# Zero matmuls in the gaps of the first batches, score pieces of one full bank, and `x` written by chunks

## The chip, the cores and the metric

One core of a Trainium2 chip runs the kernel. The metric is the time of one execution on the device in microseconds, as the median of three runs. TensorE (PE) multiplies matrices; its weight loads are listed as PEld. VectorE (DVE), ScalarE (ACT) and GpSimd (POOL) do the rest, and the queues of SyncE (SP) and ACT issue the transfers. The clock of TensorE is granted at one of two levels, 1.2 or 2.4 GHz; the profile gives the granted share (0.50 or 1.00) of every stretch.

## What is computed

Eight batches of eight heads, 576 tokens of 64 numbers each, in fp32. First a linear attention with a norm; its result, laid out with 512 numbers a token, goes into a mixture of four attention experts, of which each token uses two.

```python
kv  = einsum('bhsd,bhse->bhde', k, v)
out = einsum('bhsd,bhde->bhse', q, kv)
x   = out / sqrt(mean(out*out, -1) + 1e-6) * g_norm     # -> [B, S, 512]
logits = x @ w_gate                                     # two best of four experts, softmax over them
for e in range(4):
    q, k, v = x @ wq[e], x @ wk[e], x @ wv[e]
    a = softmax(causal(q @ k.T / sqrt(64)))
    y += gate[e] * (a @ v @ wo[e])
```

## The kernel before

A batch goes through these steps, each a small function of the kernel that emits its instructions. `kv(b, c)` multiplies k and v of two heads in twenty instructions and four such pieces make a batch; `kvx` and `kvc` copy the result out of PSUM, `kt` and `kg` multiply it with the gate weights `wg_bd`. `q(b, i)` turns q over (five tiles of tokens, the last of 64 rows; in batches 0 and 1 on TensorE, later on VectorE), `out(b, i)` is the product with `kv`. `oc` copies it to `o_sb`, `sq` squares it on ACT, `red` sums on DVE, eleven small `nw` steps on DVE find the reciprocal root, and `xm(b, i)` on POOL scales the tile into `x_tok`. `x(b, i)` turns it over on TensorE in four transposes (L585), `xc` copies it to `xT`. Then the expert projections `v` (five tiles), `qp` and `kp` (for two pairs of experts), and for each pair the scores `sc`, in pieces of one PSUM buffer each, with `exp` on ACT and a causal mask `msk` on POOL per piece; `pv` multiplies with v, `rc`, `iv` and `oc2` scale, `ot` turns over, `otc` copies, `y` multiplies with wo, `yc` copies and `st` stores. The weights of the projections are loaded by `lw` and scaled by `ws`, k, v and q by `lk`, `lv`, `lq`, the gate weights by `lg0`.

All of this is written in an order that a planner makes before the kernel is built. `graph` lists the steps with their engine, an assumed duration, their needs and their buffers; `plan` takes, step by step, the one that can start first, and of those that can start within 0.025 of each other the one with the least `urgency`: a number per kind of step in `URGENCY`, plus `PERIOD` per batch, plus single corrections in `EDGES`. The engines then run their instructions in exactly this order. `SWAP` says for which steps the engine of a copy is exchanged. PSUM is divided into two small buffers of one bank (`sm`: kv, q, kt, kg, x, v, ot, y) and three large ones of two banks (`bg`: out, qp, kp, sc, pv). A matmul that writes a buffer waits until the step that read the buffer's earlier content has ended. Six SBUF buffers (`x`) hold both `x_tok` tiles and the weights as they are loaded.

## Time and profile before

| | |
|---|---|
| median of three runs | 261.76 us (261.53 to 261.89) |
| the profiled execution | 259.49 us, its span 257.8 us |
| TensorE busy | 228.5 us (89% of the span), 2456 matmuls |
| DVE, ACT, POOL busy | 169.7, 152.5, 82.6 us |
| mean granted clock of TensorE | 0.934 |
| moved by DMA | 40.28 MB, 156 GB/s over the span |

The profile is of one execution. Matmuls are pipelined and their ends are modelled, so a busy TensorE is not one at its peak; the chain of waits, which follows the work that ended last back from the end, shows how long a step held the next one up. Names of buffers stand as output, arrow, inputs.

### The profile page before, as it was taken

Reading aid. Unit: us, or ns where it says so; the run is one execution under the profiler, and the core shown is the slowest. Engines: PE = TensorE matmul, PEld = TensorE weight load, DVE = VectorE, ACT = ScalarE, POOL = GpSimd, SP = SyncE. Lnnn points to the kernel's source line nnn. Section 1 sums busy time; section 2 is a strip of 40 time slices with the busy share of each in tenths; the row PEclk is TensorE's granted clock in tenths of the full one; section 3 lists DMA queues with packets and bytes.
Section 4 is the critical chain, followed back from the end, with each engine's and each line's share of the span. In section 5 each row is a group of like instructions: output and inputs, shape, how many; then the busy total and the mean of one; then the engine's idle time right before and its main releaser. Section 6 shows DMA issues by size and latency. Waiting matters only on the chain.

```text
span 257.8 us, 6403 instructions
## 1 busy us (share of the span) xinstructions
PE 228.5 (89%) x2456; PEld 205.5 (80%) x2456; DVE 169.7 (66%) x503; ACT 152.5 (59%) x277; POOL 82.6 (32%) x160
## 2 busy tenths in 40 slices
...
DMA packets 99432, 40.28 MB, mean 156 GB/s; under 512 B 76618, under 2 KB 94538, under 8 KB 99402
## 3 DMA queue, kind: packets, MB, share of 16 engines
...
q8 instruction: 19, 0.31, 0.6%
...
## 4 chain that ended last, share of the span: by engine, by line
PE 78%; DMA 7%; DVE 6%; ACT 4%; SPq 1%; issue 1%; POOL 0%; DVEq 0%; POOLq 0%; ACTq 0%
PE p_out L630 15%; PE p_sc L814 9%; PE p_x L585 8%; PE p_q L788 7%; PE p_kv L567 7%; PE p_y L896 7%; PE p_v L770 7%; PE p_k L788 7%; PE p_pv L848 5%; DMA q_b<-in_q_dram 3%; DMA k_b<-in_k_dram 3%; ACT PT L828 2%; PE p_ot L886 2%; DMA w_stage<-in_moe_wv_dram 2%; PE p_kg L611 1%
## 5 line engine op out<-in xcount | busy, mean ns | idle before, releaser
L834 POOL TENSOR_SCALAR_AFFINE_SELECT PT<-PT 128x256 bf16<-128x256 bf16 (+1 forms) x80 | 29.3, 384 | 126.1 <-ACT PT L828 125.0
L828 ACT ACTIVATE PT<-p_sc 128x512 bf16<-128x512 f32 (+3 forms) x80 | 50.6, 718 | 3.4 <-PE p_sc L814 3.0
L709 POOL TENSOR_TENSOR x_tok<-o_sb,rs 128x512 f32<-128x512 f32 (+1 forms) x40 | 41.2, 1049 | 19.1 <-DVE rs L685 19.0
L630 PE MATMUL p_out<-kvx,qT 128*128 128x136 f32 x320 | 44.8, 290 | 0.9 <-DVE kvx L456 0.4
L630 PEld LDWEIGHTS p_out<-kvx,qT 128*128 128x128 f32 x320 | 41.2, 197 | 2.3 <-DVE o_sb L456 0.6
L814 PE MATMUL p_sc<-qTp,kT 128*128 128x288 f32 (+4 forms) x192 | 39.0, 323 | 0.0
L656 DVE TENSOR_REDUCE ms<-sq 128x8 f32<-128x520 f32 (+1 forms) x40 | 27.1, 687 | 17.7 <-ACT sq L650 17.2
L585 PE MATMUL p_x<-ident_f,x_tok 128*128 128x128 f32 (+1 forms) x160 | 28.3, 307 | 5.2 <-POOL x_tok L709 4.1
L650 ACT ACTIVATE sq<-o_sb 128x512 f32<-128x512 f32 (+1 forms) x40 | 25.0, 634 | 11.8 <-DVE o_sb L456 9.6
L814 PEld LDWEIGHTS p_sc<-qTp,kT 128*128 128x128 f32 x192 | 28.5, 190 | 3.6 <-ACT PT L828 0.7
L567 PE MATMUL p_kv<-v_b,k_b 128*64 128x64 f32 x512 | 23.4, 242 | 8.9 <-DMA k_b<-in_k_dram 7.8
L567 PEld LDWEIGHTS p_kv<-v_b,k_b 128*64 128x64 f32 x512 | 20.0, 153 | 12.4 <-issue 11.0
L456 DVE COPY o_sb<-p_out 128x544 f32<-128x544 f32 (+1 forms) x30 | 21.4, 716 | 11.2 <-PE p_out L630 11.0
L585 PEld LDWEIGHTS p_x<-ident_f,x_tok 128*128 128x128 f32 (+1 forms) x160 | 23.1, 209 | 7.1 <-POOL x_tok L709 5.5
L770 PE MATMUL p_v<-wv_r,xT 128*128 128x256 f32 x160 | 25.7, 292 | 0.7 <-DVE vext L456 0.7
L896 PE MATMUL p_y<-wo_b,OT 128*128 128x512 bf16 x80 | 23.8, 400 | 1.0 <-ACT OT L454 0.7
L454 ACT CAST kT<-p_k 64x576 fp32r<-64x576 f32 x32 | 20.3, 634 | 4.7 <-PE p_k L788 4.2
L770 PEld LDWEIGHTS p_v<-wv_r,xT 128*128 128x128 f32 x160 | 21.6, 189 | 1.6 <-DVE vext L456 1.1
L788 PE MATMUL p_q<-xT,wq_r 128*128 128x288 f32 x128 | 21.9, 323 | 0.0
L454 ACT CAST xT<-p_x 128x512 fp32r<-128x512 f32 (+1 forms) x25 | 13.3, 545 | 14.3 <-PE p_x L585 14.2
L788 PE MATMUL p_k<-xT,wk_r 128*128 128x288 f32 x128 | 20.2, 303 | 0.0
L788 PEld LDWEIGHTS p_q<-xT,wq_r 128*128 128x128 f32 x128 | 19.3, 206 | 0.3
...
## 6 DMA issues: line engine op xcount, KB each, us to landing
...
k_b<-in_k_dram SPq DMA_DIRECT2D x14, 512.0 KB, 5.2
v_b<-in_v_dram SPq DMA_DIRECT2D x14, 512.0 KB, 7.8
...
```

Source lines behind the costliest of these rows:

```text
L454: nc.scalar.copy(dst, src)
L567: nc.tensor.matmul(p_kv[hh * Dh : (hh + 1) * Dh, c, :], lhsT=lhs, rhs=rhs, start=(j == 0), stop=(j == NF), skip_group_check=True,)
L585: nc.tensor.transpose(p_t[:, c, :nt], chunk(c)[:nt], ident_f[:nt, :nt])
L630: nc.tensor.matmul(p_o[:, c // 2, (c % 2) * 256 : (c % 2) * 256 + 2 * GW], lhsT=blocks_of(qT, c)[:, i * P : (i + 1) * P], rhs=kvx[b % 2][: ...
L656: nc.vector.tensor_reduce(mss[b % 2][:nt, i, :], sqs[(NB * b + i) % 3][:nt], axis=AX_X, op=AluOpType.add)
L709: nc.gpsimd.tensor_tensor(out=buf(("x", b, i), [P, H, Dh], FP32, "x_tok")[:nt], in0=ob[:nt, i, :, 0:Dh], in1=st["rstd", b][:nt, i * H : (i ...
L770: nc.tensor.matmul(p_v[:], lhsT=blocks_of(xTs[b % 2], c)[:, i * P : (i + 1) * P], rhs=w_r["v"][:, c, :, :].rearrange("p e f -> p (e f)"), ...
L788: nc.tensor.matmul(p_p[:, s, 0:HALF], lhsT=w_r[nm][:, c, 2 * pr : 2 * pr + 2, :].rearrange("p e f -> p (e f)"), rhs=blocks_of(xTs[b % 2], ...
L814: nc.tensor.matmul(p_s[:, el, o : o + hi - lo], lhsT=kTs[pr][el][:, kb * P : (kb + 1) * P], rhs=tiles["qTp", b, pr][:, lo:hi], start=True, ...
L828: nc.scalar.activation(PT[:, :, d0 : d0 + o], big("sc", b, pr, j)[:, :, 0:o], ACTF.Exp, scale=scale)
L834: nc.gpsimd.affine_select(out=d, in_=d, compare_op=AluOpType.is_ge, fill=0.0, base=0, pattern=[[0, 2], [1, w]], channel_multiplier=-1,)
L896: nc.tensor.matmul(p_y[:], lhsT=blocks_of(OTs[b % 2], pr)[:, qc * P : (qc + 1) * P], rhs=wo_b[:, pr, :], start=(pr == 0), stop=(pr == EP - 1),
```

## The change

TensorE gets matmuls of zeros: in the planner's order, wherever it sees a gap ahead of a TensorE step in the first 55 us, as many as fill 0.8 of that gap (0.5 in the first 10 us) are written into the PSUM tile that the step is about to use, just ahead of it. There are 79 of them: 26, 4, 4 and 7 of 256 columns ahead of the four pieces of `kv(0)`, 2, 3, 3, 3 and 3 of 512 columns ahead of the tiles of `q(0)`, 2 ahead of the first `out(0)`, 13 of 256 columns between the halves of `kv(1)`, 4 of 512 ahead of the second tile of `q(1)`, and 2 and 3 ahead of the first two tiles of `x(0)`. POOL sets a tile of zeros for them before the first. The score pieces go from five to four a pair, with 512 columns per expert in three of them and 64 in the last; the mask steps follow. `xm` writes `x_tok` so that every fourth element of a token stands in one chunk of 128, and the transposes read such a chunk. In the last batch `ot` and `otc` run in two parts, tokens 0 to 383 and 384 to 575, and each `y` tile needs only its part. Copies are swapped between DVE and ACT one by one, two of the six `ws` go to DVE, and the numbers of the order are others.

```diff
-ON_ACT = ("kvc", "xc", "qpc", "kpc", "otc", "yc")
-SWAP = {"kgc": (6,), "ktc": (1,), "kvc": (0,), "kvx": (1,), "oc": (0, 1), "otc": (1,), "qc": (1,), "qpc": (7,), "vc": (1, 6), "xc": (0, 6, 7), "yc": (0, 1, 6)}
...
+SWAP = {
+    "ws": (('q', 0), ('v', 0),), "qc": ((0, 4), (1, 0), (1, 1), (1, 3),),
+    "oc": ((0, 0), (0, 1), (1, 2), (1, 3), (1, 4), (6, 1), (6, 2), (6, 3), (7, 2), (7, 3),),
+    "xc": ((0, 0), (0, 1), (1, 0), (1, 2), (1, 4), (6, 0), (6, 2), (6, 3), (7, 2), (7, 4),),
...
+                    name, nd = ("ws", nm, p), [("lw", nm, p), ("lg0",)]
+                    (dve if swapped(name) else pool)(name, 0.60 if swapped(name) else 1.08, nd, (("x", nm, p),))
...
-            hold = (0.31, 0.31, 0.46, 0.34, 0.46)
-            took = (0.66, 0.66, 0.95, 0.72, 0.60)
...
-            for j in R5:
-                pe(("sc", b, p, j), hold[j], [("qpc", b, p), ("kpc", b, p)], (("bg", "sc", b, p, j), ("qTp", b, p)))
-                act(("exp", b, p, j), took[j], [("sc", b, p, j)] + old, (("bg", "sc", b, p, j),))
-                if j != 1:
-                    pool(("msk", b, p, j), 0.41 if j < 4 else 0.70, [("exp", b, p, j)])
+            for j in R4:
+                pe(
+                    ("sc", b, p, j), (0.47, 0.62, 0.52, 0.24)[j], [("qpc", b, p), ("kpc", b, p)],
+                    (("bg", "sc", b, p, j), ("qTp", b, p)),
+                )
+                act(("exp", b, p, j), 1.09 if j < 3 else 0.28, [("sc", b, p, j)] + old, (("bg", "sc", b, p, j),))
+                pool(("msk", b, p, j), (0.41, 0.41, 0.80, 0.36)[j], [("exp", b, p, j)])
...
+            for at in ((b, p),) if b < B - 1 else ((b, p, 0), (b, p, 1)):
+                part = at[2] if at[2:] else 2
+                pe(
+                    ("ot",) + at, (0.20, 0.14, 0.31)[part], [("oc2", b, p, g) for g in R2 if g == part or part == 2],
+                    (("sm", "ot") + at, ("osc", b, p)),
...
-COLD = 15.005
+WARM = 55.0
+COLD = 6.005
...
-PERIOD = 173.5
+PERIOD = 171.6
 URGENCY = {
-    "den": (51.7, -21.4, -19.57), "ex": (292.1, 19.87, -23.53), "exp": (295.6, -38.9, -16.04),
...
+    "den": (-113, -5.12, -28.6), "ex": (-96.9, 40.06, -25.25), "exp": (1115.2, -48.08, -0.44),
...
+            if space is psum and dtype == FP32 and len(shape) < 4:
+                t = tiles[key][:]
+                keep_warm(t if len(shape) == 2 else t.rearrange("p a b -> p (a b)"))
...
+    def keep_warm(t):
+
+        n = min(512, t.shape[1])
+        for _ in range(int(idle[0] / (n / 2400.0 + 0.01)) if n >= 256 else 0):
+            nc.tensor.matmul(t[:, 0:n], lhsT=zeros[:, 0:P], rhs=zeros[:, 0:n], start=True, stop=True, skip_group_check=True)
+        idle[0] = 0.0
...
-        p_kv = small([P, NCH, Dh], "kv", b)
+        p_kv = small([P, 2, NCH, Dh], "kv", b)
+        keep_warm(p_kv[:, 1].rearrange("p c d -> p (c d)"))
+        p_kv = p_kv[:, 0]
...
+        shape = [nt, H, Dh // NCH, NCH]
         nc.gpsimd.tensor_tensor(
-            out=buf(("x", b, i), [P, H, Dh], FP32, "x_tok")[:nt],
-            in0=ob[:nt, i, :, 0:Dh],
-            in1=st["rstd", b][:nt, i * H : (i + 1) * H].unsqueeze(2).to_broadcast([nt, H, Dh]),
+            out=buf(("x", b, i), [P, NCH, P], FP32, "x_tok")[:nt].rearrange("p c (h r) -> p h r c", h=H),
+            in0=ob[:nt, i, :, 0:Dh].rearrange("p h (r c) -> p h r c", c=NCH),
+            in1=st["rstd", b][:nt, i * H : (i + 1) * H].unsqueeze(2).unsqueeze(3).to_broadcast(shape),
...
-        t = tiles["x", b, i][:].rearrange("p h d -> p (h d)")
-        transpose_in(i, lambda c: t[:, c : c + NCH * (P - 1) + 1 : NCH], "x", b, i)
+        transpose_in(i, lambda c: tiles["x", b, i][:, c, :], "x", b, i)
...
-    PIECES = (((0, 0, HALF),), ((0, HALF, S),), ((1, P, S),), ((2, 2 * P, S),), ((3, 3 * P, S), (4, 4 * P, S)))
...
+    PIECES = (
+        ((0, 0, NF * P),), ((0, NF * P, S), (1, P, S)), ((2, 2 * P, S), (3, 3 * P, S)), ((4, 4 * P, S),),
+    )
...
-        for kb, _, _ in PIECES[j]:
+        for kb in ((0,), (1,), (2, 3), (4,))[j]:
...
+    def ot(b, pr, part=None):
+        at = (b, pr) if part is None else (b, pr, part)
+        p_t = small([P, NB * P], "ot", *at, dtype=BF16)
+        for qc in ot_part(part)[0]:
             nc.tensor.transpose(
                 p_t[:, qc * P : (qc + 1) * P], tiles["osc", b, pr][:, qc, :, :].rearrange("p e f -> p (e f)"), ident_b[:]
             )
 
-    def ot_copy(b, pr):
-        copy("otc", b, OTs[b % 2][:, pr * S : (pr + 1) * S], small(None, "ot", b, pr)[:, 0:S])
+    def ot_copy(b, pr, part=None):
+        at = (b, pr) if part is None else (b, pr, part)
+        _, lo, hi = ot_part(part)
+        copy(("otc",) + at, OTs[b % 2][:, pr * S + lo : pr * S + hi], small(None, "ot", *at)[:, lo:hi])
...
-    tasks = graph(B)
+    free = 0.0
     with tc.manual_schedule():
-        for _, _, n in plan(tasks, POOLS, {n: urgency(n) for n in tasks})[0]:
+        for t, _, n in plan(tasks, POOLS, {n: urgency(n) for n in tasks})[0]:
+            if tasks[n][0] == "PE":
+                idle[0] = (0.5 if t < 10.0 else 0.8) * (t - free) if t < WARM else 0.0
+                free = t + tasks[n][1]
             emit[n[0]](*n[1:])
+            idle[0] = 0.0
```

SP's queue from the sixth transfer on, before: `w_stage` are the weights of the projections, `wo_st` those of the output, `k_b`, `v_b`, `q_b` the inputs of batch 1.

```order
L540 DMA w_stage<-in_moe_wq_dram 128x2x256 x2
L540 DMA w_stage<-in_moe_wk_dram 128x2x256 x2
L540 DMA w_stage<-in_moe_wv_dram 128x2x256 x2
L555 DMA wo_st<-in_moe_wo_dram 128x512 x2
L493 DMA k_rem_83<-in_k_dram 64x8x64
L493 DMA v_rem_85<-in_v_dram 64x8x64
L481 DMA k_b<-in_k_dram 128x4x256
L481 DMA v_b<-in_v_dram 128x4x256
L481 DMA k_b<-in_k_dram 128x4x256
L481 DMA v_b<-in_v_dram 128x4x256
L505 DMA q_b<-in_q_dram 128x8x64 x4
L505 DMA q_b<-in_q_dram 64x8x64
```

And now:

```order
L593 DMA wo_st<-in_moe_wo_dram 128x512 x2
L530 DMA k_rem_83<-in_k_dram 64x8x64
L530 DMA v_rem_85<-in_v_dram 64x8x64
L518 DMA k_b<-in_k_dram 128x4x256
L518 DMA v_b<-in_v_dram 128x4x256
L518 DMA k_b<-in_k_dram 128x4x256
L518 DMA v_b<-in_v_dram 128x4x256
L542 DMA q_b<-in_q_dram 128x8x64 x4
L542 DMA q_b<-in_q_dram 64x8x64
L577 DMA w_stage<-in_moe_wv_dram 128x2x256 x2
L577 DMA w_stage<-in_moe_wk_dram 128x2x256 x2
L530 DMA k_rem_74<-in_k_dram 64x8x64
```

The inputs of batch 1 moved ahead of the weights of v and k; those of q come another six transfers later, behind k and v of batch 2.

ACT from its first `oc` of batch 0 on, before (`o_sb<-p_out` is `oc`, `sq` is `sq`):

```order
L454 COPY o_sb<-p_out 128x544
L650 ACTIVATE sq_94<-o_sb 128x8x64
L454 COPY o_sb<-p_out 128x544 x2
L650 ACTIVATE sq_96<-o_sb 128x8x64
L454 COPY o_sb<-p_out 128x544
L650 ACTIVATE sq_98<-o_sb 128x8x64
L454 COPY o_sb<-p_out 64x544
L650 ACTIVATE sq_94<-o_sb 128x8x64
L650 ACTIVATE sq_96<-o_sb 64x8x64
```

And now, from `kvc(0)` on:

```order
L491 COPY kvc_80<-p_kv 128x256
L491 COPY qT<-p_q 128x4x64
L491 COPY o_sb<-p_out 128x544
L690 ACTIVATE sq_94<-o_sb 128x8x64
L491 COPY o_sb<-p_out 128x544
L690 ACTIVATE sq_96<-o_sb 128x8x64
L690 ACTIVATE sq_98<-o_sb 128x8x64
L690 ACTIVATE sq_94<-o_sb 128x8x64
L690 ACTIVATE sq_96<-o_sb 64x8x64
L491 COPY kvx_87<-p_kv 64x4x64 x2
```

Three of the five copies of `out(0)` have left ACT; they stand on DVE between its reductions.

TensorE from `x(0)` on, before: `p_x` are transposes of x, `p_q<-ident_f` those of q, `p_q<-xT` the projection of batch 0.

```order
L585 MATMUL p_x<-ident_f,x_tok 128x128 x8
L567 MATMUL p_kv<-v_b,k_b 64x64 x8
L567 MATMUL p_kv<-v_rem_85,k_rem_83 64x64 x2
L567 MATMUL p_kv<-v_b,k_b 64x64 x8
L567 MATMUL p_kv<-v_rem_85,k_rem_83 64x64 x2
L585 MATMUL p_x<-ident_f,x_tok 128x128 x4
L601 MATMUL p_kt<-ident_f,kvc_89 128x128 x2
L585 MATMUL p_x<-ident_f,x_tok 128x128 x4
L611 MATMUL p_kg<-wg_bd,kvT 128x16 x2
L585 MATMUL p_x<-ident_f,x_tok 128x64 x4
L585 MATMUL p_q<-ident_f,q_b 128x128 x4
L788 MATMUL p_q<-xT_108,wq_r 128x288 x16
```

And now, behind the second tile of `x(0)`:

```order
L625 MATMUL p_q<-ident_f,q_b 128x128 x4
L670 MATMUL p_out<-kvx_87,qT 128x136 x4
L625 MATMUL p_x<-ident_f,x_tok 128x128 x4
L670 MATMUL p_out<-kvx_87,qT 128x136 x4
L625 MATMUL p_q<-ident_f,q_b 128x128 x4
L625 MATMUL p_x<-ident_f,x_tok 128x128 x4
L670 MATMUL p_out<-kvx_87,qT 128x136 x4
L625 MATMUL p_q<-ident_f,q_b 128x64 x4
L811 MATMUL p_v<-wv_r,xT_110 128x256 x4
L670 MATMUL p_out<-kvx_87,qT 128x136 x4
L625 MATMUL p_x<-ident_f,x_tok 128x64 x4
L811 MATMUL p_v<-wv_r,xT_110 128x256 x4
```

The tiles of `out(1)` and `q(1)` moved in among those of `x(0)`, the projection of q behind them, and `kv(1)` ahead of them.

## Rows read from the trace of the kernel before

**Rows 1.** The page, part 4: shares of the chain that ended last, by engine.

```profile
PE 78%; DMA 7%; DVE 6%; ACT 4%; SPq 1%; issue 1%; POOL 0%; DVEq 0%; POOLq 0%; ACTq 0%
```

**Rows 2.** Stretches: length, busy time of PE, PEld, DVE, ACT, POOL, granted clock.

```profile
15.57:22.40 6.83, 3.62 (x16) 2.90 (x17) 4.80 (x12) 1.49 (x2) 0.00 (x0) 0.50 0.78 186
...
22.40:25.81 3.41, 1.67 (x14) 1.46 (x14) 1.94 (x8) 0.00 (x0) 1.12 (x2) 1.00 0.94 282
...
36.05:53.12 17.07, 13.65 (x87) 11.85 (x88) 6.34 (x24) 2.92 (x7) 5.09 (x5) 0.50 1.05 219
...
53.12:245.20 192.08, 190.36 (x2132) 174.61 (x2131) 144.58 (x426) 138.45 (x251) 64.02 (x115) 1.00 0.60 134
```

**Rows 3.** Chain of waits in order of time: start, length, step, count.

```profile
25.07 4.73 PE p_out L630 x24
...
37.05 1.09 POOL x_tok L709
...
49.29 3.84 PE p_q L788 x16
...
53.13 0.93 PE p_q L585 x8
...
54.99 0.83 PE p_q L585 x8
...
59.72 2.48 PE p_kv L567 x80
...
62.87 2.11 PE p_k L788 x16
...
84.36 0.95 PE p_v L770 x8
...
85.31 0.93 PE p_out L630 x8
...
99.86 0.56 PE p_x L585 x4
...
104.33 0.96 PE p_x L585 x8
...
106.22 0.62 PE p_x L585 x4
...
249.04 0.65 ACT OT L454
```

**Rows 4.** Chain of waits of the first 60 us alone.

```profile
23.65 0.25 DVE wg_bd L532
```

**Rows 5.** Timeline of PE, ACT, DVE: start, length, engine, line, operation, count.

```profile
7.44 1.12 PE L567 MATMUL p_kv<-v_b,k_b 128*64 128x64 f32 x16 [7.44 <-DMA k_b<-in_k_dram]
...
12.29 0.30 PE L567 MATMUL p_kv<-v_rem,k_rem 128*64 128x64 f32 x4
...
26.61 0.61 ACT L454 COPY o_sb<-p_out 128x544 f32<-128x544 f32 x1 [7.07 <-PE p_out L630]
...
27.26 0.63 ACT L650 ACTIVATE sq<-o_sb 128x512 f32<-128x512 f32 x1
...
33.05 1.29 DVE L656 TENSOR_REDUCE ms<-sq 128x8 f32<-128x520 f32 x2 [0.32 <-ACT sq L650]
```

**Rows 6.** Groups by shape: busy us, mean ns of one, idle before.

```profile
L709 POOL TENSOR_TENSOR x_tok<-o_sb,rs 128x512 f32<-128x512 f32 x32 | 33.2, 1052 | 19.1 <-DVE rs L685 19.0
...
L828 ACT ACTIVATE PT<-p_sc 128x576 bf16<-128x576 f32 x32 | 20.0, 671 | 0.3 <-PE p_sc L814 0.3
...
L456 DVE COPY o_sb<-p_out 128x544 f32<-128x544 f32 x24 | 17.2, 720 | 11.0 <-PE p_out L630 10.8
...
L828 ACT ACTIVATE PT<-p_sc 128x896 bf16<-128x896 f32 x16 | 14.9, 932 | 1.0 <-PE p_sc L814 0.8 <-POOL PT L834 0.2
```

**Rows 7.** Timeline of SP's queue, 38 to 60 us.

```profile
41.24 13.50 SPq L508 DMA_DIRECT2D q_b<-in_q_dram  x8
```

**Rows 8.** Transfers by line: count, KB each, median us from issue to landing.

```profile
v_b<-in_v_dram SPq DMA_DIRECT2D x14, 512.0 KB, 7.8
```

More of the change, by code (lines that the diff above doesn't have):

```diff
@@ L54, in dve, with copy @@
         add(name, "DVE", took - 0.05, took + 0.05, needs, tiles)
-    def copy(name, on_act, on_dve, needs, tiles=()):
-        if engine_of(name) == "ACT":
-            act(name, on_act, needs, tiles)
-        else:
-            dve(name, on_dve, needs, tiles)
     def pool(name, took, needs, tiles=()):
         add(name, "POOL", took - 0.03, took + 0.10, needs, tiles)
+    def copy(name, on_act, on_dve, needs, tiles=(), first=dve):
+        ways = ((dve, on_dve), (act, on_act))
+        if first is act:
+            ways = ways[::-1]
+        make, took = ways[swapped(name)]
+        make(name, took, needs, tiles)
     R5, R4, R2 = range(NB), range(NCH), range(EP)
@@ L345 @@
     tiles = {}
+    tasks = graph(B)
+    idle = [0.0]
     def buf(key, shape, dtype, name):
@@ L387 @@
     nc.gpsimd.memset(ob[REM:P, NF], 0.0)
+    zeros = const.tile([P, 512], BF16, name="zeros")
+    nc.gpsimd.memset(zeros[:], 0.0)
     zrow = const.tile([P, P], FP32, name="zrow")
@@ L450, in head, with copy @@
         return 2 * c + hh if b < QPE else NCH * hh + c
-    def copy(kind, b, dst, src):
-        if engine_of((kind, b)) == "ACT":
+    def copy(task, dst, src):
+        if tasks[task][0] == "ACT":
             nc.scalar.copy(dst, src)
@@ L545, in ws @@
     def ws(nm, p):
-        nc.gpsimd.tensor_tensor(
+        eng = nc.gpsimd if tasks["ws", nm, p][0] == "POOL" else nc.vector
+        eng.tensor_tensor(
             out=w_r[nm][:, :, 2 * p : 2 * p + 2, :].rearrange("p c e f -> p e c f"),
@@ L572, in kvx_copy @@
     def kvx_copy(b):
-        p_kv = small(None, "kv", b)
+        p_kv = small(None, "kv", b)[:, 0]
         for hh in range(2):
             pp = slice(hh * Dh, (hh + 1) * Dh)
-            copy("kvx", b, kvx[b % 2][pp, :, hh, 0:Dh], p_kv[pp, :, :])
+            copy(("kvx", b), kvx[b % 2][pp, :, hh, 0:Dh], p_kv[pp, :, :])
     def kvc_copy(b):
-        copy("kvc", b, kvcs[b % 2][:], small(None, "kv", b)[:])
+        copy(("kvc", b), kvcs[b % 2][:], small(None, "kv", b)[:, 0])
     def transpose_in(i, chunk, *key):
@@ L595, in q_copy @@
         nt = blocks[i][1]
-        copy("qc", b, tokens(qT, i), small(None, "q", b, i)[:, :, :nt])
+        copy(("qc", b, i), tokens(qT, i), small(None, "q", b, i)[:, :, :nt])
     def kt(b):
@@ L605, in kt_copy @@
     def kt_copy(b):
-        copy("ktc", b, buf(("kvT", b), [P, EP, P], FP32, "kvT")[:], small(None, "kt", b)[:])
+        copy(("ktc", b), buf(("kvT", b), [P, EP, P], FP32, "kvT")[:], small(None, "kt", b)[:])
     def kg(b):
```

59 lines of the change are left out of this document (35 added, 24 removed), and 40 rows, old and new, of tables (EDGES, SWAP, URGENCY).

## The prediction

> **What bounds the kernel now.** I read the shares of the chain of waits first: TensorE carries 78% of the chain that ended last [rows 1]. Then the stretches cut where the granted clock changes [rows 2]. From 53.12 us to 245.20 us the matmul engine is busy for 190.36 of 192.08 us at 2.4 GHz: that stretch gets shorter only if its matmuls cost less or if some of them are done before it begins. Ahead of it the clock was granted at 0.50 (1.2 GHz) for 17.07 us, and the engine was busy for 13.65 of those. So there are two prices: work that enters the long stretch earlier, and cheaper work inside it. Third, the chain in order of time [rows 3] shows what ends last at the start: the gate weights' product at 23.65 [rows 4], batch 0's `out` at 25.07, its normalisation until the POOL product `xm` at 37.05, then transposes and projections at half clock until batch 2's `kv` at 59.72.
>
> **Start, until `xm` of batch 0.** `out(0)` needs `kgc`, that needs `wg_bd`, and `wg_bd` is written at 23.65 when its small loads land [rows 4]. The change leaves these loads on the same queue in nearly the same place, so `out(0)` cannot begin much before 25. The new zero matmuls must fit in front of it. Forty-one of 256 columns stand around the four `kv(0)` pieces (26 ahead of the first), 14 of 512 columns among the `q(0)` transposes and 2 ahead of `out(0)`. A matmul of 256 columns takes 0.95/8 = 0.12 us at 2.4 GHz [rows 3] and I take 0.24 at 1.2 (288 columns took 3.84/16 there, same rows). Before, `kv(0)` began at 7.44 at the slow rate, 16 in 1.12 us, and the last four, at 12.29, ran faster [rows 5]. If the zeros begin at 7.4 as well and the clock rises at 12.2 again, 20 run slowly and 6 fast: 4.8 + 0.7 = 5.5, until 12.9. Then 15 zeros (1.8) and 80 `kv` instructions (2.48, rows 3) end at 17.2, and 14 zeros of 512 columns (0.24 each, 3.4) with five transposed tiles (4 x 0.465 + 0.37, below) at 22.8; copies between them add about a microsecond. That is just the 23.65 of the gate weights: I charge 0.2 us. With every zero at 1.2 GHz the charge would be 26 x 0.12 + 15 x 0.12 + 14 x 0.24 = 8.3 less the 1.5 us of slack, about 6; with all fast it is nothing.
>
> Behind `out(0)`, ScalarE did five copies and five squares, 0.61 and 0.63 each, from 26.61, and the last two reductions on VectorE began at 33.05 and took 1.29 [rows 5]. After the change ScalarE has two copies, VectorE three at 0.72 [rows 6]. VectorE then sets the end: first tile at 25.3 + 1.1, copy and square 1.24, then five reductions at 0.65 to 0.69 and three copies, 5.6, end at 33.2 where it was 34.34. `xm(0)` begins at 35.9, 1.15 earlier.
>
> **From `xm(0)` to `kv(2)`.** Weights now load behind batch 1's inputs, so batch 1's `out` stands among batch 0's `x` transposes, ahead of the projections. I count TensorE's work in the new order from the first `x` transpose, 35.9 + 1.09 [rows 3], to `kv(2)`, at 2.4 GHz: `out(1)` 5 x 0.93 = 4.65; `x(0)` 4 x 0.465 + 0.37 = 2.2; three tiles of `q(1)` 1.3; `kg` 0.35; `v(0)` 5 x 0.475 = 2.4; `kp(0)` 2.1; three zeros 0.65 [rows 3]. Sum 13.65 (that it equals the busy time above is chance), so `kv(2)` at 50.7. POOL permits that: four `xm`, three weight products and a fifth `xm`, 8 x 1.05 [rows 6], end at 44.3, with 4.95 of the listed work behind it, 49.3. Before, `kv(2)` began at 59.72, without `v(0)` and `kp(0)` (4.5 more work after) but with `qp(0)` (2.1 less; it costs as `kp`). Lead at equal work: 59.7 - 50.7 + 2.3 = **11.3 us**. It is kept to the end, since the stretch behind it is TensorE-bound in both kernels. Zeros that lie in waits cost nothing; the cover is gone where data come earlier than planned, and then one costs 0.12 or 0.24.
>
> The bounds of this term are the clock and the loads. If the clock stays at 1.2 GHz (16 projection matmuls then take 3.84 us against 2.11 [rows 3]), the 13.65 becomes about 25 and the lead is nothing. If the loads permit more, up to 13.5 us: `q(2)` was issued from 41.24 for 13.50 us [rows 7].
>
> What the trace says of transposes and the clock: from 15.57 to 22.40 TensorE ran 16 matmuls at 0.50, nearly all fp32 transposes, and 1.00 was granted for 22.40 to 25.81 [rows 2]. The Trainium skill (TensorE: Matmul & The Clock Gate, Part 4) says that transposes do not count as busy for the full clock; by that rule the new stretch, half of it transposes, would stay slow, as in the first rival; the rise at 22.40 speaks against it.
>
> **`x` by chunks.** The transposes of `x` read every fourth element as weights; now 128 in a row, as `q`'s do. Two `q` tiles take 0.93 at 2.4 GHz, 0.465 each, and a full with a 64-row tile 0.83, so 0.37 for the small one. `x` takes 0.96 for two or 0.56 for one, and 0.62 for the small one [rows 3]. A batch gains 4 x (0.015 to 0.095) + 0.25 = 0.31 to 0.63; 0.45 for batches 1 to 7 is **3.2 us** (batch 0 is counted above). Bounds: nothing, if the step is not the cause, and 4.4.
>
> The price is on POOL, whose write now steps by 512 bytes. No row shows such a write; a plain one takes 1.05 us [rows 6]. I take 1.05, since all that changes is where the same 512 elements go; bounds 1.05 to 2.1, and a gain is excluded since nothing is left out. The Trainium skill (GPSIMD Engine Reference, 7. Performance pitfalls for Q7 kernels) gives half as much again per element for reads that step over 8 bytes. Were writes like that, `xm` would take an estimated 1.55 us, and the sum with it would be some 4 to 8 us worse. No row here shows it.
>
> **Score pieces.** Columns are the same (3,200 a pair) and so is the number of matmuls. ScalarE has four `exp` instead of five. Widths 576 and 896 took 671 and 932 ns [rows 6], 0.816 per column, so 1,024 takes an estimated 1.04 and 128 about 0.3: 3.4 a pair, where the five were 3.6. ScalarE is not the bound, but a large PSUM buffer is now held 0.1 longer per piece, and there are four handovers instead of five. Taken at nothing; bounds -3 (0.19 x 16 pairs, all exposed) and +1.7 (0.1 x 16).
>
> **Tail.** The whole `ot` copy took 0.65 from 249.04 [rows 3], behind both halves of the scaling. By halves, the first `y` tiles wait for the short half alone: about 0.3 of copy and 0.6 of waiting less. **0.9 us**; bounds 0 and 1.6.
>
> **Sum.** 11.3 + 3.2 + 0.9 = 15.4. The profiled execution took 259.49 (span 257.8), so 244.1; the median shown is 261.76, 2.3 above it, and the same difference gives **246.4 us**.
>
> **Rivals.**
> 1. The clock is not held between 37 and 51 us. For: the engine was busy 13.65 of 17.07 us and got 0.50 [rows 2]. Against: the rise at 22.40, and zeros now fill the gaps. Lead nothing, 261.8 - 3.2 - 0.9 = 257.7. Chance 0.10.
> 2. Loads take over: batch 2's `kv` and batch 3's are wanted 9 to 18 us earlier. Before, `v(2)` was issued just ahead of 41.24 [rows 7] and such a load lands after 7.8 [rows 8], so at about 49, and one weight load of three now follows it; it is wanted at 50.7. There is a margin of some 2 us, and `kv(3)` stands close behind `out(2)`. If 3 us of the lead are lost: 249.5. Chance 0.20.
> 3. The step was not what made `x` slow, so that part does not do what it says: 246.4 + 3.2 = 249.6. For: pairs of tiles differ by only 0.03. Chance 0.07.
> 4. Slower than before: the stepped write makes `xm` long. In the new order POOL runs all five `xm` of a batch in one piece ahead of the masks, so `x`, and the `pv` behind the masks, come late. Exposed in all eight batches, 15.4 us are used up at 15.4/40 = 0.39 per `xm`, that is from 1.44 us on; at 2.1 us, half exposed, it gives 246.4 + 40 x 1.05/2 = 267. For: no row shows the write. Against: POOL is idle most of the time in the long stretch, 64.02 busy of 192.08 [rows 2]. Chance 0.07.
>
> **Numbers.** The forecast itself has 0.56. The range reaches down to 240.5 (loads permitting 13.5, `x` at 4.4, some of the score pieces' 3) and up to 255, which takes in rivals 2 and 3 and a clock held in half of the stretch; it leaves out rivals 1 and 4. About 0.2% (0.5 us) is what a measurement of this kernel can tell from no change. Faster 0.92, same 0.01, slower 0.07.
>
> **What would show it.** Right: a granted clock of 1.00 without a fall between about 30 and 245 us; `kv(2)` near 51; the first `xm` near 36 and at 1.05; `x` tiles at 0.47 and the small one below 0.4 in the chain; the stretch at full clock about as busy as before. Wrong: 0.50 in that stretch; TensorE waiting for `k_b`, `v_b` or `q_b` after 45 us; `xm` over 1.4 us; the first `kv(0)` so late that `out(0)` starts behind 27. The forecast fails most easily on the count of 13.65 us without a gap: it takes every copy between two small PSUM buffers to be in time.

## The result, and the profile after

The changed kernel takes 253.08 us (median of four runs) against 261.64 us for the kernel before on the same chip; the ratio is 0.967, 95% interval 0.957 to 0.977. A second measurement gave 250.86 against 259.68, ratio 0.966 (0.961 to 0.971). So some 8.7 us were gained where 15.4 were forecast; the predicted 246.4 us was not reached, and the time lies within the range of 240.5 to 255.0. The profiled execution took 251.83 us (span 250.1); before it was 259.49 (257.8). The difference that the traces have to explain is therefore 7.7 us.

First the clock. These are the busy times by stretch of the changed kernel, core 0; behind the length of the stretch stand busy time and number of instructions of TensorE, its weight loads, VectorE, ScalarE and GpSimd, then the granted clock, the share of the DMA engines and GB/s:

```profile
12.40:55.11 42.71, 37.73 (x402) 31.53 (x401) 27.38 (x70) 15.38 (x29) 9.36 (x9) 1.00 1.09 227
55.11:150.00 94.89, 94.02 (x1163) 86.75 (x1163) 78.19 (x230) 63.42 (x110) 34.47 (x59) 1.00 1.07 210
150.00:240.80 90.80, 85.39 (x928) 76.57 (x926) 69.94 (x195) 65.50 (x111) 29.99 (x56) 1.00 0.20 67
240.80:250.10 9.30, 3.85 (x20) 1.44 (x20) 1.44 (x6) 4.41 (x9) 0.00 (x0) 0.88 0.52 186
```

The same cuts in the kernel before, at the same points of the work: the first `kv(2)` at 59.72 there and 55.11 here, the end of the last `pv` at 247.11 there and 240.80 here:

```profile
7.44:59.72 52.28, 38.19 (x330) 34.13 (x332) 22.81 (x65) 16.06 (x31) 11.86 (x13) 0.74 1.08 226
59.72:155.00 95.28, 94.57 (x1158) 87.15 (x1158) 76.91 (x226) 64.31 (x117) 32.89 (x59) 1.00 0.95 205
155.00:247.11 92.11, 91.10 (x953) 82.57 (x952) 68.03 (x206) 68.06 (x124) 31.53 (x57) 1.00 0.19 63
247.11:257.80 10.69, 4.61 (x21) 1.62 (x19) 1.98 (x8) 4.09 (x7) 0.00 (x0) 0.69 0.45 160
```

The last `pv` of the kernel before, that of the second pair of experts, in TensorE's timeline:

```profile
246.04 1.07 PE L848 MATMUL p_pv<-vext,PT 128*128 128x65 bf16 x30
```

Three readings follow. First, the clock is 1.00 throughout from 12.4 us to the tail, where it was 0.50 from 36 to 53 us before [rows 2]. Second, from `kv(2)` to the last `pv` the changed kernel is only 1.7 us faster, 185.69 against 187.39 us, although TensorE is busy for 6.3 us less there: its idle time in that part has grown, 0.87 + 5.41 us against 0.71 + 1.01. Third, the tail is shorter by 1.4 us.

The start in the chain of waits of the changed kernel (start, length, engine and line; it answers to [rows 3]):

```profile
15.30 3.92 DMA wg_st<-in_moe_w_gate_dram
...
19.24 0.75 ACT L428
...
20.74 0.27 ACT kvc L491
...
21.05 0.81 PE p_q L386 x3
...
27.44 4.90 PE p_out L670 x40
...
33.65 1.52 PE p_kv L386 x13
...
37.31 0.59 ACT qT L491
...
37.94 1.02 PE p_q L386 x4
...
39.44 0.59 ACT qT L491
...
40.08 0.59 PE p_x L386 x2
40.67 0.45 PE p_x L625 x4
...
55.18 0.84 PE p_kv L607 x23
```

`out(0)` begins at 27.44, not at 25.3. In front of it ScalarE copies `kvc` at 20.74, behind the activation table load (L428) and behind the issues of the gate weights' loads; the second `q(0)` tile needs the PSUM buffer that this copy frees, and TensorE stood idle for 2.66 us until 21.05. The diff had moved `kvc(0)` from VectorE to ScalarE.

The largest idle time later on is one of 2.17 us. The order of time on three engines around it (start, length, engine, line, instruction; in brackets the idle time before and its releaser):

```profile
191.23 5.07 POOL L751 TENSOR_TENSOR x_tok<-o_sb,rs 128x512 f32<-128x512 f32 x5
...
192.74 3.93 DVE L776 TENSOR_TENSOR sh<-lg,m 128x20 f32<-128x20 f32 x1
...
196.59 0.68 DVE L493 CAST xT<-p_x 128x512 fp32r<-128x512 f32 x1
...
197.42 0.84 PE L625 MATMUL p_x<-ident_f,x_tok 128*128 128x128 f32 x6 [2.17 <-DVE mk L785]
```

`sh` is a subtraction of 20 numbers a partition. Here it took 3.93 us, until the row of five `xm` on GpSimd had ended; the copy of `x` out of PSUM stood behind it on VectorE, and the next transposes behind the copy.

### The profile page after: what moved, and what is told of

It reads as the page before. It is cut to its first block, busy times and chain, and to the rows that moved or that the text cites. A ratio compares the mean times of both kernels' runs of the same rounds, so it can differ in the third digit from the quotient of the medians.

```text
span 250.1 us, 6517 instructions
## 1 busy us (share of the span) xinstructions
PE 226.6 (91%) x2535; PEld 200.0 (80%) x2535; DVE 181.1 (72%) x510; ACT 148.7 (59%) x258; POOL 81.3 (32%) x159
## 4 chain that ended last, share of the span: by engine, by line
PE 76%; DMA 8%; ACT 7%; DVE 6%; issue 1%; ACTq 1%; DVEq 0%
PE p_out L670 14%; PE p_sc L858 9%; PE p_v L811 8%; PE p_kv L607 7%; PE p_k L829 7%; PE p_q L829 7%; PE p_x L625 6%; PE p_pv L892 6%; PE p_y L948 6%; ACT PT L872 3%; DMA q_b<-in_q_dram 3%; DMA v_b<-in_v_dram 2%; DVE sh L776 2%; PE p_ot L936 2%; PE p_q L386 2%; DMA wg_st<-in_moe_w_gate_dram 2%
## 5 line engine op out<-in xcount | busy, mean ns | idle before, releaser
L872 ACT ACTIVATE PT<-p_sc 128x128 bf16<-128x128 f32 (+1 forms) x64 | 51.4, 849 | 8.3 <-PE p_sc L858 7.9
L858 PE MATMUL p_sc<-qTp,kT 128*128 128x64 f32 (+4 forms) x192 | 39.8, 335 | 0.6 <-ACT PT L872 0.4
L690 ACT ACTIVATE sq<-o_sb 128x512 f32<-128x512 f32 (+1 forms) x40 | 25.3, 637 | 18.0 <-DVE o_sb L493 15.5
L811 PE MATMUL p_v<-wv_r,xT 128*128 128x256 f32 x160 | 26.5, 296 | 2.2 <-DVE xT L493 1.5
L625 PE MATMUL p_x<-ident_f,x_tok 128*128 128x128 f32 (+1 forms) x160 | 21.9, 267 | 2.5 <-DVE mk L785 2.2
L625 PEld LDWEIGHTS p_x<-ident_f,x_tok 128*128 128x128 f32 (+1 forms) x160 | 17.1, 141 | 4.9 <-issue 3.2
L491 ACT CAST xT<-p_x 128x512 fp32r<-128x512 f32 (+1 forms) x30 | 15.7, 546 | 8.9 <-PE p_x L625 8.8
L386 PEld LDWEIGHTS <-zeros 128*128 128x128 bf16 x79 | 8.6, 116 | 15.5 <-POOL zeros L424 6.8
L607 PE MATMUL p_kv<-v_b,k_b 128*64 128x64 f32 x512 | 20.1, 225 | 0.0
L491 ACT COPY y<-p_y 128x512 f32<-128x512 f32 (+1 forms) x31 | 17.8, 593 | 3.8 <-PE p_y L948 2.5
L607 PEld LDWEIGHTS p_kv<-v_b,k_b 128*64 128x64 f32 x512 | 17.6, 138 | 2.6 <-issue 1.5
L829 PE MATMUL p_q<-xT,wq_r 128*128 128x288 f32 x128 | 19.2, 300 | 0.0
```

The costliest lines, as they stand in the source:

```text
L491: nc.scalar.copy(dst, src)
L607: nc.tensor.matmul(p_kv[hh * Dh : (hh + 1) * Dh, c, :], lhsT=lhs, rhs=rhs, start=(j == 0), stop=(j == NF), skip_group_check=True,)
L625: nc.tensor.transpose(p_t[:, c, :nt], chunk(c)[:nt], ident_f[:nt, :nt])
L811: nc.tensor.matmul(p_v[:], lhsT=blocks_of(xTs[b % 2], c)[:, i * P : (i + 1) * P], rhs=w_r["v"][:, c, :, :].rearrange("p e f -> p (e f)"), ...
L829: nc.tensor.matmul(p_p[:, s, 0:HALF], lhsT=w_r[nm][:, c, 2 * pr : 2 * pr + 2, :].rearrange("p e f -> p (e f)"), rhs=blocks_of(xTs[b % 2], ...
L858: nc.tensor.matmul(p_s[:, el, o : o + hi - lo], lhsT=kTs[pr][el][:, kb * P : (kb + 1) * P], rhs=tiles["qTp", b, pr][:, lo:hi], start=True, ...
```

## The experiments

Unless said otherwise an edit is made to the changed kernel and keeps its order on every engine. "Before" in the ratios is the kernel before, run on the same chip in turn with the others.

| | us | ratio to before (95%) |
|---|---|---|
| changed kernel, second measurement | 250.86 | 0.966 (0.961 to 0.971) |
| without zeros | 256.03 | 0.985 (0.981 to 0.990) |
| without the first 26 zeros | 253.90 | 0.974 (0.969 to 0.979) |
| `kvc(0)` on VectorE | 249.65 | 0.962 (0.958 to 0.965) |
| late gate steps | 249.04 | 0.959 (0.956 to 0.963) |
| both of these | 246.57 | 0.950 (0.946 to 0.955) |
| both, no zeros in `kv(1)` | 248.36 | 0.956 (0.952 to 0.960) |
| both, no zeros behind `out(0)` | 248.32 | 0.957 (0.953 to 0.961) |
| both, `ot` of the last batch whole | 247.75 | 0.954 (0.950 to 0.957) |
| both, five y buffers | 245.58 | 0.946 (0.942 to 0.952) |
| `x` token by token | 255.02 | 0.983 (0.978 to 0.988) |
| kernel before with zeros | 256.85 | 0.989 (0.984 to 0.995) |

The interval of the changed kernel overlaps those of `kvc(0)` on VectorE, of the late gate steps and of the kernel without the first 26 zeros, and that of both edits overlaps those of the four kernels made from it. What such a step is worth is read from the traces, one profile of each kernel.

**The changed kernel once more.**

> The changed kernel itself once more, as the measure for the others on the same chip. Both theories: 251 to 253.5 us, kv(2) at 55.1, idle times of TensorE of 2.17 us near 195 and 1.49 near 217. Whether the granted clock falls behind the first of these (it fell to 0.50 for 3.41 us there in three kernels with that wait and not in the first profile of the changed one) is left to the run: with a fall some 1.7 us more.

250.86 us. `kv(2)` began at 56.11, an idle time of 2.16 us stood at 196.25 and none of 1.49 near 217. TensorE's wait for `kvc(0)` was 3.53 us here, and the clock was at 0.50 from 20.1 to 23.5 us behind it; `out(0)` began at 28.44. So two profiles of one kernel differ by 1.0 us at `out(0)` and, from `kv(2)` to the last `pv`, by 1.2 us (184.52 here).

**Without any zeros.** The theory is that of the forecast: zeros hold the clock, and the clock makes the lead. The rival: the new order does.

```diff
-        n = min(512, t.shape[1])
+        n = 0
```

> The changed kernel without its 79 zero matmuls; every other instruction stays, in the same order on every engine. Theory (the zeros hold the clock): the granted clock is 1.00 only from about 22 to 26 us, falls to 0.50 around 35 us as before the change, and the transposes, out(1), v(0) and kp(0) between 37 and 55 us run at half rate: kv(2) begins at 62 to 66 us instead of 55.2 and the time is 259 to 263 us. Rival (the new order alone made the gain, and the work itself would hold the clock): no stretch at 0.50 after 30 us, kv(2) within 1 us of 55.2, time 251.5 to 254.

256.03 us, between the two. Its stretches:

```profile
27.31:30.73 3.42, 3.42 (x18) 3.42 (x17) 0.69 (x1) 1.95 (x4) 0.00 (x0) 0.50 1.15 276
30.73:40.97 10.24, 7.66 (x119) 6.64 (x118) 8.96 (x29) 4.44 (x9) 2.25 (x3) 1.00 0.99 225
40.97:47.79 6.82, 5.26 (x25) 5.21 (x25) 4.33 (x10) 0.65 (x3) 4.83 (x5) 0.50 0.96 291
47.79:57.73 9.94, 9.94 (x83) 9.38 (x82) 7.44 (x15) 6.34 (x13) 2.20 (x3) 1.00 1.37 157
```

The clock does fall without the zeros, at 40.97 behind gaps of TensorE of 0.87 and 1.60 us at 36.3 and 37.8, but the work alone brings it back, at 30.73 and at 47.79. `kv(2)` begins at 57.73, 2.6 us later than with zeros. So of the lead at equal work (6.9 us, worked out below) the zeros make 2.6 us and the order 4.3.

**Zeros alone, in the old order.** The kernel before gets the same rule for zeros and nothing else: the functions of the diff around `keep_warm`, the second half of the `kv` bank, and `idle` in the loop.

```diff
+            if tasks[n][0] == "PE":
+                idle[0] = (0.5 if t < 10.0 else 0.8) * (t - free) if t < 55.0 else 0.0
+                free = t + tasks[n][1]
             emit[n[0]](*n[1:])
+            idle[0] = 0.0
```

> The kernel before, in its old order, with zero matmuls by the same rule (0.5 of a planned gap ahead of 10 us, 0.8 until 55 us), and nothing else of the change. Theory (the clock is most of the lead): 1.00 from 12 us without a fall, kv(2) at 54 to 56 us instead of 59.72, time 254 to 256 us. Rival (the order is most of it: without zeros the changed kernel began kv(2) only 2.6 us later): kv(2) at 57 or later, time 257 to 259.5.

256.85 us, 1.1% less than before, and `kv(2)` at 58.64, 1.0 us earlier (59.65 in the same view): the rival. From 9.5 us on the clock was 1.00 but for 26.5 to 29.9 us. But `out(0)` began 3.1 us later than before, at 28.16, and the zeros are not what TensorE waited for: it stood for 3.31 us until the four `wg_bd` steps on VectorE had ended. These began at 23.58, where they had begun at 23.26 before, but took 0.79 to 1.08 us each instead of 0.21 to 0.23, in a stretch in which `ws` ran on GpSimd:

```profile
23.30 2.04 POOL L560 TENSOR_TENSOR wq_r<-w_stage,g_rows 128x512 fp32r<-128x512 f32 x2 [14.72 <-DMA g_rows<-in_g_norm_dram]
...
24.29 1.08 DVE L547 TENSOR_SCALAR wg_bd<-wg_sp,g_wide 64x16 f32<-64x16 f32 x1
...
26.51 1.00 PE L627 MATMUL p_kg<-wg_bd,kvT 128*128 128x16 f32 x4 [3.31 <-DVE wg_bd L546]
```

In the kernel before `ws` began at 24.69, behind them:

```profile
23.26 0.21 DVE L532 TENSOR_SCALAR wg_bd<-wg_st,g_wide 64x16 f32<-64x16 f32 x1
```

Between `out(0)` and `kv(2)` this kernel gained 4.1 us (30.48 against 34.58). So the 1.0 us at `kv(2)` is not the price of the zeros in the old order: some 3 us for the slow steps are in it (that `ws` slowed them is read from the order of time and was not tried), and this profile, 258.29 us, is the slowest of four runs. Still the price that I put on the clock (rival 1, the whole lead of 11.3) was too high in either order.

**The first 26 zeros left out.**

```diff
-                idle[0] = (0.5 if t < 10.0 else 0.8) * (t - free) if t < WARM else 0.0
+                idle[0] = (0.0 if t < 10.0 else 0.8) * (t - free) if t < WARM else 0.0
```

> The changed kernel without the zeros planned before 10 us, which are the 26 ahead of the first piece of kv(0); the other 53 stay. Theory (those 26 are hidden behind the wait of q(0) for the copy kvc(0) on ScalarE, which ended at 20.99): kv(0) begins at 7.4 instead of 12.46, the second q(0) tile still begins at 21, out(0) at 27.4 and the time stays within 0.5 us of 253.1. Rival (they delay the start): out(0) begins 1.5 to 2.5 us earlier and the time is 251 or less.

253.90 us, and both theories miss: `out(0)` came later, at 29.72. `kv(0)` was done early, TensorE stood for 5.32 us until 21.05 for the same `kvc` copy, which ended when it had before, and behind this longer gap the `q(0)` tiles ran at half clock:

```profile
18.89:25.72 6.83, 4.67 (x16) 2.78 (x16) 0.90 (x2) 1.75 (x3) 0.00 (x0) 0.50 0.76 227
```

In the traces the 26 zeros bring `out(0)` forward by 1.3 to 2.3 us (28.44 and 27.44 in the two profiles with them), not by filling the gap but by making it shorter; the times leave it open, since the intervals overlap.

**`kvc(0)` on VectorE.** If the gap is the trouble, the copy should not stand behind the table load.

```diff
-        copy(("kvc", b), kvcs[b % 2][:], small(None, "kv", b)[:, 0])
+        copy(("kvc" if b else "kvx", b), kvcs[b % 2][:], small(None, "kv", b)[:, 0])
...
+    order = plan(tasks, POOLS, {n: urgency(n) for n in tasks})[0]
+    names = [o[2] for o in order]
+    order.insert(names.index(("kvx", 0)) + 1, order.pop(names.index(("kvc", 0))))
```

> The changed kernel with the one copy kvc(0) on VectorE, right behind kvx(0), instead of on ScalarE, where it stood behind eight DMA issues and the activation table load. Theory: TensorE's wait of 2.66 us at 18.4 is gone, out(0) begins at 25.3 to 25.8 instead of 27.44 (the gate weights' loads come next), and about all of that reaches the end: 250.5 to 251.8 us. Rival (batch 0's start is not what sets kv(2); loads or the copies of q(1) do): out(0) earlier, but kv(2) still at 54.5 or later and a time within 0.7 us of 253.1.

249.65 us. The wait has shrunk to 0.43 us, `out(0)` begins at 25.01 and `kv(2)` at 52.69, 2.4 us earlier than in the changed kernel's first profile. In its own profile part of this is given back later: behind the idle time of 2.17 us, at 192.89 here, the clock fell for 3.41 us.

```profile
192.89:195.06 2.17, 0.00 (x1) 0.03 (x1) 2.15 (x3) 0.71 (x2) 2.17 (x6) 1.00 0.31 121
196.29:199.70 3.41, 3.41 (x17) 3.41 (x16) 2.58 (x6) 1.87 (x5) 0.77 (x2) 0.50 0.02 5
```

Such a fall stood behind this idle time in four of six profiles (no zeros, no first zeros, this one, `x` token by token), not in the two of the changed kernel. It costs up to half of 3.41, 1.7 us, so the wait is dearer than its own length.

**The gate steps behind the copies of `x`.** The theory: `sh` and its like read two operands from SBUF while `xm` runs. The edit moves seven small steps of three batches in VectorE's order, one of them in ScalarE's.

```diff
+    for b in (5, 6, 7):
+        for group, after in ((("sh", "ex", "mk"), 0), (("gt", "den", "rd", "gate"), 16)):
+            held = [o for o in order if o[2][0] in group and o[2][1] == b]
+            order = [o for o in order if o not in held]
+            at = max(k for k, o in enumerate(order) if o[2][:2] in (("xc", b), ("mk", b))) + 1 + after
+            at = min([at] + [k for k, o in enumerate(order) if o[2][:2] == ("iv", b)])
+            order[at:at] = held
```

> The changed kernel with the seven gate steps (sh, ex, mk, gt, den, rd, gate) of batches 5, 6 and 7 written behind that batch's last copy of x, so that no two-input VectorE step meets the row of five xm on GpSimd. Theory (sh at 169.76 took 1.79 us and at 192.74 3.93 us instead of 0.17 because xm was running, the copies of x stood behind it and TensorE behind them): the idle times of TensorE of 0.69 at 167.8 and 2.17 at 195.25 go, sh takes 0.17 to 0.5, time 250.0 to 251.2 us. The wait at 217.2 (behind the inv step at 215.10) is not touched and stays. Rival (TensorE then waits as long for something else, masks or ScalarE): 252.4 or more, with idle times of the same sum after 150 us.

249.04 us. The same place in the order of time, now without a wait: the copy of `x` no longer waits for the row of `xm`, and TensorE no longer for the copy.

```profile
191.32 5.12 POOL L751 TENSOR_TENSOR x_tok<-o_sb,rs 128x512 f32<-128x512 f32 x5
...
193.56 0.69 DVE L493 CAST xT<-p_x 128x512 fp32r<-128x512 f32 x1 [0.77 <-PE p_x L625]
...
195.18 1.04 PE L625 MATMUL p_x<-ident_f,x_tok 128*128 128x128 f32 x8
```

`sh` over its eight batches, of the changed kernel and of this one (shortest, median, longest in ns):

```profile
L776 DVE TENSOR_TENSOR sh<-lg,m x8: 136/344/3932, 40.0 to 213.0; 128x20 f32<-128x20 f32 x8
```
```profile
L776 DVE TENSOR_TENSOR sh<-lg,m x8: 138/170/661, 39.5 to 216.6; 128x20 f32<-128x20 f32 x8
```

From `kv(2)` to the last `pv` it takes 183.35 us (54.60 to 237.95) where the changed kernel took 185.69 and 184.52 in its two profiles. Two details of the expectation were wrong. The 0.69 us at 167 stayed, so they have another cause. And the 1.49 us near 217 went, where the `inv` step took 1.04 instead of 2.50 us; but it was missing in the second profile of the changed kernel too, with an `inv` of 1.13, so that this edit removes it is not shown. In place of the 2.17 us stands a new idle time of 0.79 us, at 170.19.

**Both edits.**

> The changed kernel with kvc(0) on VectorE behind kvx(0) and with the late gate steps of batches 5 to 7, that is both single edits together. Theory (the two losses lie in different places and add up): kv(2) at 52.7, no idle time above 1 us after 100 us, no fall of the clock before the end, 246.0 to 247.5 us. Rival (the earlier start is eaten by the same later waits): 248.5 or more.

246.57 us, within the theory's range: as far as the intervals can tell, they add up. The start in its chain of waits:

```profile
16.68 0.43 DVE kvx L493
...
17.12 0.43 DVE kvc L493
...
24.00 4.90 PE p_out L670 x40
...
51.74 0.27 PE p_kv L607 x4
```

No idle time above 0.8 us is left between 45 us and the tail, and the clock does not fall before it. `kv(2)` lies 1.0 us ahead of that with the first edit alone (52.69), and that is not the edits' doing: the first `kv(0)` began at 11.25 here and at 12.26 there, since the 26 zeros ahead of it took 4.52 and 5.51 us.

**Fewer zeros behind `out(0)`.** In the chain of the changed kernel zeros of 1.52, 1.02, 0.59 and 0.81 us stand between `out(0)` and the second tile of `x(0)`. The first edit drops the 13 of `kv(1)`, the second all behind `out(0)`.

```diff
-        keep_warm(p_kv[:, 1].rearrange("p c d -> p (c d)"))
+        b == 0 and keep_warm(p_kv[:, 1].rearrange("p c d -> p (c d)"))
```
```diff
-WARM = 55.0
+WARM = 25.0
```

> The kernel with both single edits (kvc(0) on VectorE, late gate steps; 246.57 us) without the 13 zeros ahead of the third piece of kv(1). Theory (these zeros stand on the chain: the loads they were to wait for had come, and they took 1.53 us): x(0) begins at 35.7 to 36.2 instead of 37.08, the clock stays at 1.00, 245.0 to 245.8 us. Rival (without them the gaps behind kv(1) bring the clock to 0.50 for a time, as in the kernel without any zeros): 246.6 or more.

> The kernel with both single edits, with zeros only up to out(0): the 13 of kv(1), the 4 of q(1) and the 2 and 3 of x(0) are left out. Theory (zeros in a gap that is a wait for the same PSUM buffer come after the wait, not in it, and cost their own 1.53 + 1.02 + 0.59 + 0.81 us less what the copies still take): x(0) at 35.7, kv(2) at 48.5 to 50 instead of 51.67, clock 1.00 throughout, 243.5 to 245.0 us. Rival (these zeros are what holds the clock between 33 and 45): 0.50 there, kv(2) at 51 or later, 246 or more.

248.36 and 248.32 us, and the traces have what the rivals said, a fall of the clock and a later `kv(2)`; by the times alone a loss is hardly clear of the noise. `x(0)` began earlier in the second, at 35.97 against 37.08, but the clock fell:

```profile
37.58:44.41 6.83, 5.72 (x26) 5.75 (x27) 4.27 (x10) 1.08 (x2) 4.83 (x6) 0.50 1.11 281
```

In the first it fell from 38.99 to 42.41, and `kv(2)` began at 54.01, in the second at 54.07 (51.67 with all zeros; 0.9 and 0.2 of the difference are a later first `kv(0)`). Zeros that stand on the chain here do buy the clock behind it, and without them the chain goes over VectorE anyway: TensorE waited 1.47 and 1.56 us for the copy of the first tile of `x(0)`.

**`x` token by token.** `xm` and the transposes as in the kernel before.

```diff
-        transpose_in(i, lambda c: tiles["x", b, i][:, c, :], "x", b, i)
+        t = tiles["x", b, i][:].rearrange("p h d -> p (h d)")
+        transpose_in(i, lambda c: t[:, c : c + NCH * (P - 1) + 1 : NCH], "x", b, i)
```

> The changed kernel with x written token by token again and transposed with every fourth element as weights; same order. Theory (the step is what makes x slow; 0.435 against 0.48 for a full tile and 0.39 against 0.62 for the small one in the chains, 0.41 a batch, eight batches): weight loads of x at 0.21 instead of 0.14 us, 2.5 to 3.5 us more than the changed kernel. Rival (the layout does not matter): within 0.6 us. GpSimd's xm starts every 1.00 us in either layout by both.

255.02 us, 1.7% or 4.4 us more than the changed kernel by the ratios (the intervals leave some 2 us either way). From `kv(2)` to the last `pv` TensorE is busy with the transposes of `x` for 22.01 us, and for 19.07 in the changed kernel: 2.9 us. Weight loads, matmuls and `xm` (ns), of this kernel and then of the changed one:

```profile
L625 PEld LDWEIGHTS p_x<-ident_f,x_tok x160: 192/210/259, 41.2 to 222.3; 128*128 128x128 f32 x128, 64*128 64x128 f32 x32
L625 PE MATMUL p_x<-ident_f,x_tok x160: 270/284/386, 41.4 to 222.4; 128*128 128x128 f32 x128, 64*128 64x64 f32 x32
L749 POOL TENSOR_TENSOR x_tok<-o_sb,rs x40: 1032/1038/1178, 39.0 to 220.3; 128x512 f32<-128x512 f32 x32, 64x512 f32<-64x512 f32 x8
```
```profile
L625 PEld LDWEIGHTS p_x<-ident_f,x_tok x160: 134/140/223, 40.3 to 216.9; 128*128 128x128 f32 x128, 64*128 64x128 f32 x32
L625 PE MATMUL p_x<-ident_f,x_tok x160: 221/272/328, 40.5 to 217.0; 128*128 128x128 f32 x128, 64*128 64x64 f32 x32
L751 POOL TENSOR_TENSOR x_tok<-o_sb,rs x40: 1059/1110/1297, 38.0 to 215.1; 128x512 f32<-128x512 f32 x32, 64x512 f32<-64x512 f32 x8
```

Weight loads with the step take 0.21 instead of 0.14 us, as expected. `xm` is listed 72 ns longer with the stepped write, but the five in a row above (5.07 us) start every 1.00 us, as in the plain layout: the step costs GpSimd nothing that anyone waits for.

**The last batch's `ot` in one piece.** Made to the kernel with both edits, by exchanging `b < B - 1` for `b < B` at the two places of the graph.

> The kernel with both single edits, with ot of the last batch copied and waited for as a whole again. Theory (the tail term, 0.9 by the forecast): 0.3 to 0.9 us more than 246.57, the copy of ot 0.65 instead of 0.33 and 0.49 in the chain. Rival (the last y copies wait 2.4 us for a y buffer whose store has not ended, whatever ot does): within 0.2 us.

247.75 us. The chain of waits at the end, whole and then by halves:

```profile
237.34 0.47 PE p_ot L936 x5
237.83 0.65 ACT OT L491
...
239.81 2.36 DMA out_dram<-y
```
```profile
235.91 0.28 PE p_ot L936 x2
...
236.21 0.33 ACT OT L491
...
236.93 0.49 ACT OT L491
...
238.01 2.38 DMA out_dram<-y
```

From the end of the last `pv` to the end of the span it is 10.25 us (235.75 to 246.0) against 9.24 (234.96 to 244.2): the halves are worth 1.0 us in the traces.

**Five y buffers.** Both chains above end in a wait for a store that frees a y buffer. The edit adds a buffer and gives two of the last five copies to VectorE.

```diff
-            tiles[key] = space.tile(shape, dtype, tag=key[0], name=name, bufs=POOLS[key[0]])
+            tiles[key] = space.tile(shape, dtype, tag=key[0], name=name, bufs=POOLS[key[0]] + (key[0] == "y"))
...
-        copy(("yc", b, qc), buf(("y", b, qc), [P, D], FP32, "y")[:nq, :], small(None, "y", b, qc)[:nq, :])
+        copy(("yc", b, qc) if b < B - 1 or qc % 2 == 0 else ("oc2", b, 0, 0), buf(("y", b, qc), [P, D], FP32, "y")[:nq, :], small(None, "y", b, qc)[:nq, :])
```

> The kernel with both single edits (246.57 us), with five y buffers instead of four and the second and fourth y copy of the last batch on VectorE. Theory (at the end the last y copy waits 0.51 us on ScalarE for the store from the buffer it is to use, and ScalarE alone makes five copies of 0.59): the last copy ends near 239.8 instead of 241.08, 245.2 to 245.8 us. Rival (the stores behind them are what ends last): within 0.3 us of 246.57.

245.58 us, the fastest kernel of the study. But the tail itself went only from 9.24 to 9.01 us (235.59 to 244.6), so the mechanism that I gave for the last copy is worth about 0.2, and that this kernel is faster than the one with both edits is not shown by the overlapping intervals.

## Why the prediction was right in direction and half right in size

**Start until `xm(0)`: wrong by 2.1 us.** `out(0)` began at 27.44 instead of 25.3 and `xm(0)` at 38.05 instead of 35.9. I charged the zeros 0.2 us and took the gate weights for the only thing in front of `out(0)`. The diff moved one copy, `kvc(0)`, to ScalarE, whose queue was issuing the gate weights' loads until 19.2 and then loading its table. I counted "copies between them" as about a microsecond without asking on which engine each stands. With that copy on VectorE `out(0)` began at 25.01, so the 25.3 was right for the rest, but in part by luck: the gate weights, which I named as the bound, did not hold it up. In that run `kg` followed at 23.94 on the last tile of `q(0)` without a gap, so what came true is the other count, TensorE's work until 22.8 and a microsecond of copies. Nor does [rows 4] show the loads as the last to come in the kernel before: the first `wg_bd` step began at 23.26, as VectorE's copies of `qT` ended. The wrong sign that I named, `out(0)` behind 27, is what came.

**From `xm(0)` to `kv(2)`: 14.6 us for the counted 13.65.** The weak point that I named, a count without a gap, was there but small: one wait of 0.43 us for a copy. The rest of the 0.95 us is work that took longer than counted, 0.68 us instead of 0.475 for each of the first two tiles of `v(0)` and 0.52 instead of 0.35 for `kg`. Another 1.4 us was lost ahead of it: `x(0)` began at 40.51, 13.1 us behind `out(0)` and not 11.7, because zeros and copies of `kv(1)` and `q(1)` stand between. The lead at equal work was 59.72 - 55.11 + 2.3 = 6.9 us, not 11.3; the 4.4 that lack are 2.1 + 1.4 + 0.95.

**Clock: right, for half a reason.** It stayed at 1.00 through all the transposes between 40 and 52 us. Rival 1 did not come, but its price was wrong: without any zeros the order alone keeps 4.3 us of the lead. The Trainium skill (TensorE: Matmul & The Clock Gate, Part 4) says that the full clock does not engage for transposes in TensorE's transpose mode, so by it that stretch would have been slow; this trace does not bear that out, at 1.00 from 12.4 to 240.8 us, though it lists these transposes as MATMUL and does not show the mode.

**"Kept to the end": wrong by 4.6 us.** This is the other term that failed. I took the long stretch as bound by TensorE in both kernels, since it was busy for 190.36 of 192.08 us [rows 2]. In the changed kernel idle time there rose from 1.7 to 6.3 us (5.2 in its second profile). Moving the gate steps alone took 2.3 us off this part against the first profile and 1.2 against the second, so a quarter to a half of the 4.6 is shown to come from small steps such as `sh` waiting out a row of `xm`. That the 1.49 us behind `inv` have the same cause is read from the order of time alone, and the rest has no shown cause. The place is the one that I named in rival 4, five `xm` in one piece, with the wrong mechanism: not a slow `xm`, but an engine beside it that has to wait. In the kernel before `xm` came in rows of four at most, and a small two-input step beside one was lengthened five times, to 0.60 to 0.96 us. The Trainium skill (SBUF — State Buffer, Who interferes with whom) says that a `tensor_tensor` with both inputs in SBUF contends with GpSimd's reads, and that the ports that the two share are an exclusive lock. The trace agrees, and the step waited for more than the one `xm` of 1.0 us that was running: 3.93 us for a step of 0.17. The forecast did not ask where the new order puts these steps.

**`x` by chunks: right.** 3.2 us and some 0.4 for batch 0 were forecast, 4.4 measured with an uncertainty of about 2; the step is the cause (rival 3 falls), and the write costs nothing (rival 4 falls). Of the estimate of 1.55 us that the Trainium skill's rule for reads (GPSIMD Engine Reference, 7. Performance pitfalls for Q7 kernels) would have given for a write (half more than 1.05 is 1.58), nothing is seen: 1.00 from start to start.

**Score pieces: left open.** `exp` took 1.02 (1,024 columns) and 0.27 us (128), as estimated. What the pieces did to TensorE was not tried alone; the sum below leaves 1.1 us for all that is not named.

**Tail: right.** 0.9 was forecast for the halves, and 1.0 is what they are worth. The tail as a whole shrank by 1.4 us. The other 0.4 was not tried; the mean clock there rose from 0.69 to 0.88, which speaks for a part of it.

**Rival 2 (loads): did not come.** No wait of TensorE for a load stands in the trace behind 41 us.

The sum in the traces: 6.9 (lead) + 2.9 (seven batches of `x` at 0.41, the difference of the tiles in the chains with and without the step) + 1.4 (tail) - 4.6 (new idle time) = 6.6, against 7.7 measured; 1.1 us, busy time of TensorE between `kv(2)` and the last `pv`, stay unexplained. With the two failed terms mended in part by one copy and one group of small steps, the kernel took 246.57 us. That this is nearly the 246.4 of the forecast is in part luck: on that chip the kernel before took 259.68 us, so the gain was 13.1 us of the 15.4.

Two small sums of the prediction do not come out: 8.3 less the 1.5 of slack is 6.8, not about 6, and the work moved ahead, 4.5 less 2.1, is 2.4, not 2.3. The forecast does not change by more than 0.1.
